# Attention block on one core: the third form of a row's bits made in place by an accumulating transfer from POOL, with 6 row buffers and 70 rows

## The chip, the core and the metric

The kernel runs on one core of a Trainium2 chip. The core has a matrix engine (PE, whose weight loads the profile lists apart as PEld), a vector engine (DVE), an engine for functions such as exp (ACT), a general engine (POOL) and an engine that only issues transfers (SP). Each runs its own list of instructions strictly in order, and before an instruction it can wait on semaphores that other engines or transfers raise. The metric is the device time of one execution in microseconds (us).

## The reference

The block is multi-head attention without a mask: 2048 positions, width 448, 16 heads of 28, all in bf16.

```
qkv = x @ wqkv                       # x: 2048 x 448, wqkv: 448 x 1344
q, k, v = split into 16 heads of 28
scores = q @ k^T * 28 ** -0.5        # per head 2048 x 2048
p = softmax(scores)
o = p @ v
return concat(o) @ wo                # wo: 448 x 448
```

## The kernel before

**Units, rows and tiles.** The work is cut into 16 units: a group g of four heads times a chunk c of 512 queries. A unit u walks over 16 blocks kt of 128 keys, and "row" r = 16u + kt is one such block: four tiles, one per head, each of 128 keys by 512 queries. There are 256 rows and 1024 tiles. For each tile PE computes scores into one bank of the PSUM memory (line 904, names S for groups of tiles and SD for single ones); then exp is taken; then PE multiplies the result with V and adds it up in one bank over the unit's 16 rows (line 871, names PV). A column of ones in V gives the softmax denominators. Four such products of a row, one per head, run side by side; they are called a pass here.

**Two ways to take exp.** Most rows go through ACT (line 966, names E): groups of 3 and 2 tiles alternate, over banks 0 to 2 and 3 to 4, and the results land in a ring PT of 43 slots. The rows listed in `PLAN["rows"]`, 67 of them, go through DVE instead. There exp is made from bits. Line 928 (names D1) clamps a tile's scores, adds a constant and writes 16-bit integers into a buffer DY whose bits, read as fp16, are a coarse exp. To even out the coarse error, line 936 (names DS0 and DS1) makes two more forms of the whole row by adding the integers 344 and 682, into DS. The row's product with V then has three terms in three passes: DY with V, the first DS with VW0 and the second DS with VW1, where VW0 and VW1 are V scaled by 101/128 and 80/128 (line 859). Such a row's four score tiles sit in banks 5 to 7, which also hold the accumulator and serve projections and outputs. Rows rotate through 3 buffers DY and 3 pairs DS.

**What sets the order.** The program is written as a list of operations with dependencies, priorities and guessed durations, and a list scheduler (`_Prog.schedule`) fixes each engine's order before the kernel is built. On PE every pass of products with V names the one before it in `after`, so that passes run in the order of the rows and terms. Where the scheduler sees PE falling idle it adds passes with zeros (line 484, name Z).

**Start and end.** POOL first fills parts of V, the padded `wop` and ONE with constants (lines 492 to 495); DVE makes the identity `id_b` and SEL (lines 460, 462 and 496) for the transposes of x (line 538). After a unit, its accumulator is copied (line 723) and normalised through a round trip of small transfers (lines 729 to 739). The last unit is normalised on PE and DVE (lines 778 to 839): two half copies (line 801), N1 (line 809), N2 (line 824), and the output projection of the last four tiles of positions in parts, OPA (line 789) and OPB (line 834). The output projections of other tiles of the last group (OP, line 710) are mixed in before.

Of the kernel before, what the change touches and what calls it, by code (L numbers as in the profile page):

```python
# [7 lines left out]
ALU = mybir.AluOpType  # L8
# [4 lines left out]
I16 = mybir.dt.int16  # L13
# [50 lines left out]
class _Prog:  # L64
# [272 lines left out]
PHASE = (0, 344, 682)  # L337
# [3 lines left out]
ZLO = -ZADD  # L341


CFG = {"late": 4.5, "load": 1.5, "load0": 18, "dcost": 2.3, "dlead": 30.385592406, "aslack": 235.147215477, "opp": 0.0, "oload": 2.5, "klead": 0.405674492, "vlag": 0.024622608, "hot1": 45000.0, "hotm": 3600.0, "nslack": 2585.717981114, "dlook": 20.0, "plook": 471.074451806, "rcost": 4.9, "rlead": 1.0, "rend": 4, "rgap": 2, "acost": 0.4455, "dprio": 0.651412491, "nride": 4, "rslack": 300.0, "stail": 24, "jprio": -0.750113813, "sdlap": 4.771128299, "vwlead": 1.249363626, "sdpen": 6.528606395, "rcostx": -0.000676632}

PLAN = {
    "rows": [9, 14, 16, 24, 26, 28, 33, 38, 41, 50, 53, 54, 57, 61, 62, 70, 72, 77, 80, 84, 88, 95, 97, 98, 103, 107, 109, 111, 113, 117, 123, 125, 131, 135, 138, 139, 141, 148, 149, 152, 162, 163, 164, 165, 169, 176, 177, 179, 180, 187, 189, 190, 193, 199, 200, 207, 211, 212, 213, 215, 222, 229, 231, 234, 235, 244, 248],
    "late": [1.281070854, 1.964014751, 1.915657661, 0.76, 2.743900482, 1.159356603, 1.904466413, 1.845975994, 2.106524837, 2.189415295, 2.428349574, 2.873971098, 2.728623137, 3.84085501, 2.733578841, 4.131340808, 3.508351422, 5.446684044, 4.832243098, 4.46548081, 5.163206443, 7.002171665, 6.90767575, 7.804407036, 4.947925744, 6.78739139, 5.302922841, 6.89552453, 9.777227448, 10.389677342, 7.735503962, 7.490566717, 8.23514301, 7.360578973, 7.83742904, 10.319692841, 8.329224918, 8.680463746],
}


def _fast(nc, x, wqkv, wo, out, n_heads=16):
# [12 lines left out]
    NQT = QCH // 128  # L365
    HC = H * 32
    GD = 4 * DH
    NPT = 43
    NDR = 3
    NDS = 3  # L370
    NPH = len(PHASE)
    NMENG = "dve"
    NOB = 4
# [14 lines left out]
    with es:  # L388
        def sb(name, shape, dt):
            return es.enter_context(nc.sbuf_tensor(name, shape, dt))  # L390
# [13 lines left out]
        DS = sb("DS", [128, NPH - 1, NDS, 2048], I16)  # L404
# [20 lines left out]
        def i32v(ap):  # L425
            return ap.bitcast(I32)
# [65 lines left out]
        ms_v0 = P.add("pool", lambda e: e.memset(V4[:, :, DH:32], 0.0), dur=1500, prio=-9, name="ms_v0")  # L492
        ms_v1 = P.add("pool", lambda e: e.memset(V4[:, :, VONE:VONE + 1], 1.0), deps=[ms_v0], dur=800, prio=-9, name="ms_v1")
        ms_wop = P.add("pool", lambda e: e.memset(i32v(wop.rearrange("p g d -> p (g d)")), 0), dur=900, prio=-8, name="ms_wop")
        ms_one = P.add("pool", lambda e: e.memset(ONE[:, :], 1.0), dur=100, prio=-7, name="ms_one")
        sel_op = P.add("dve", (lambda e: e.tensor_copy(SEL[:, :], id_f.rearrange("p (h r) -> p h r", r=32)[:, :, VONE])),
                       deps=[id_f_op], dur=100, prio=-6, name="sel")
# [344 lines left out]
        def pv(u, kt):  # L842
            g, c = units[u]
            r = u * NK + kt
            if r in n_row:
                ri = n_row[r] % NDR
                rk = n_row[r] % NDS
                terms = [DY[:, ri, :]] + [DS[:, k, rk, :] for k in range(NPH - 1)]
                parts = [[t_.bitcast(FP16)[:, h * 512:(h + 1) * 512] for h in range(4)] for t_ in terms]
                deps_of = [row_ops[r]] + [[o_] for o_ in row_ev[r]]  # L850
                slots = []
            else:
                slots = [tile_slot[(u, kt, h)] for h in range(4)]
                parts = [[PT[:, pi * 512:(pi + 1) * 512] for _, pi in slots]]
                deps_of = [list({id(tile_ev[(u, kt, h)]): tile_ev[(u, kt, h)] for h in range(4)}.values())]

            if r in n_row and (g, kt // 4) not in vw_ev:
                c4 = kt // 4
                vw_ev[(g, c4)] = [P.add("dve", (lambda e, k=k: e.tensor_scalar(VW[:, g % 2, k, 4 * c4:4 * c4 + 4, :], V[:, 4 * c4:4 * c4 + 4, g * 128:(g + 1) * 128],
                                                                              WTERM[k + 1], None, ALU.mult)),  # L860
                                        deps=[v_ev[(g, c4)], vw_used.get((g % 2, c4))], dur=200, prio=u + kt / NK - CFG["vwlead"], name=f"VW{k}_{g}_{c4}")
                                  for k in range(NPH - 1)]

            def weights(k, h):
                return V[:, kt, (4 * g + h) * 32:(4 * g + h + 1) * 32] if k == 0 else VW[:, g % 2, k - 1, kt, 32 * h:32 * h + 32]

            def f_pv(e, k, p_):
                ins = None
                b = pv_open[u].banks[0]
                for h in range(4):  # L870
                    ins = e.matmul(ps[32 * h:32 * h + 32, b * 512:(b + 1) * 512], weights(k, h), p_[h], start=(kt == 0 and k == 0), stop=(kt == NK - 1 and k == len(parts) - 1), tile_position=(0, 32 * h))  # L871
                return ins
            base_pr = (u - 60.0 if u == NU - 1 and kt >= NK - 3 else u + (kt + 4) / NK)
            for k, p_ in enumerate(parts):
                first, fin = kt == 0 and k == 0, kt == NK - 1 and k == len(parts) - 1
                op = P.add("pe", (lambda e, k=k, p_=p_: f_pv(e, k, p_)), deps=deps_of[k]
                           + [v_ev[(g, kt // 4)] if k == 0 else vw_ev[(g, kt // 4)][k - 1]], acq=(("M", 1) if first else None),
                           after=[last_pv[0]], kind="c", units=1.0, act=512.0, acc=(True if first else False if fin else None), prio=base_pr, name=f"PV{u}_{kt}" + (f"_{k}" if k else ""))
                last_pv[0] = op
                if first:  # L880
                    pv_open[u] = op
                if r in n_row:
                    row_pv[(n_row[r], k)] = op
                    if k:
                        vw_used[(g % 2, kt // 4)] = op
            for s_ in slots:
                slot_last[s_] = op
            if kt == NK - 1:
                (last_unit if u == NU - 1 else post_unit)(u, op)

        last_pv = [None]
        pv_next = 0
        done = set()
# [17 lines left out]
        def row_tile(r, h, partner, p_pr):  # L911
# [7 lines left out]
            old = row_pv.get((n_row[r] - NDR, 0))  # L919
            prev_row = row_at.get(n_row[r] - NDR, [])  # L920
# [5 lines left out]
            hold.append(s)  # L926
            s.ride = True
            o1 = P.add("dve", (lambda e, ri=ri, h=h, s=s: e.tensor_scalar(DY[:, ri, h * 512:(h + 1) * 512], bank(s.banks[0]), ZLO, ZADD, ALU.max, ALU.add)),  # L928
                       deps=[s, old] + prev_row, dur=600, prio=-90.0, name=f"D1_{r}_{h}", rel=[(s, 0)])
# [4 lines left out]
            rk = n_row[r] % NDS  # L934
            assert n_row[r] < NDS or (n_row[r] - NDS, 1) in row_pv, "DVE rows too close"
            row_ev[r] = [P.add("dve", (lambda e, k=k: e.tensor_scalar(DS[:, k, rk, :], DY[:, ri, :], float(PHASE[k + 1]), None, ALU.add)),  # L936
                               deps=row_ops[r] + [row_pv.get((n_row[r] - NDS, k + 1))], dur=600, prio=pr + 0.001 * k, name=f"DS{k}_{r}") for k in range(NPH - 1)]
            row_at[n_row[r]] = row_ev[r]
            done.update(4 * r + j for j in range(4))

        row_ev = {}
        row_at = {}
        for gi, (kind, idx, b0) in enumerate(items):
            tl = [tiles[i] for i in idx]
            w = len(tl)
# [32 lines left out]
            if todo_rows and 4 * todo_rows[0] - CFG["dlead"] <= idx[-1] and (nxt < NDS or (nxt - NDS, NPH - 1) in row_pv):  # L978
# [773 lines left out]
```

## Time and profile before

| | before |
|---|---|
| median of 3 runs | 362.63 us (362.26 to 363.6) |
| the profiled execution | 362.26 us, of which the span of instructions is 360.4 us |
| POOL busy | 3.4 us in 9 instructions, the last ending before 5 us |
| transfers | 9.91 MB, mean 27 GB/s over the span |
| granted PE clock | 1.000 |

The profile page gives for each engine the time with work in it (overlapping instructions counted once), the span in slices, the chain of waits that ended last, and groups of instructions with their mean duration. Queries of the trace give the same for stretches of the span, the instructions in order of time, and who waited for whom.

### The profile page before, as it was taken

The numbers are of one execution on the slowest core, as the hardware profiler recorded it, in microseconds if no ns is written. First come the engines' busy times: TensorE is split into PE (matmuls) and PEld (weight loads), VectorE is DVE, ScalarE is ACT, GpSimd is POOL, SyncE is SP. The second block draws the span as 40 slices with busy tenths as digits, with TensorE's granted clock in tenths as the row PEclk, the third lists the DMA queues.
The fourth block names the chain that finished last, engine by engine and source line by source line (L and its number), as shares of the span: only waits on it lengthen the run. The fifth ranks groups of instructions, "written<-read, shape, count | busy, mean of one in ns | idle before, by whom it ended". The sixth has DMA issues, their size and how long they took to land.

```text
span 360.4 us, 8848 instructions
## 1 busy us (share of the span) xinstructions
PE 342.2 (95%) x3885; PEld 114.4 (32%) x3885; DVE 321.8 (89%) x574; ACT 345.5 (96%) x307; POOL 3.4 (1%) x9
## 2 busy tenths in 40 slices
PE   8999999999999999999999999999998989999996
PEld 4444322332223243223333323332222222234323
DVE  6579999798999999999999998999999999999504
ACT  2999999999999999999999999999999999999992
POOL 3000000000000000000000000000000000000000
PEclk9999999999999999999999999999999999999999
DMA  8600000100100000000000000000000001010201
GB/s 232 152 2 3 2 32 5 32 2 3 33 0 5 32 18 17 2 32 3 20 15 5 31 2 32 3 14 22 29 4 3 20 15 32 16 44 28 78 29 54
DMA packets 13940, 9.91 MB, mean 27 GB/s; under 512 B 7504, under 2 KB 12048, under 8 KB 13896
## 3 DMA queue, kind: packets, MB, share of 16 engines
q1 hardware_dynamic: 13096, 8.74, 8.4%
q8 instruction: 31, 0.51, 0.6%
q10 hardware_dynamic: 800, 0.56, 0.5%
q14 instruction: 13, 0.11, 0.1%
HBM read 7.23 MB, written 2.06 MB: 26 GB/s over the span
## 4 chain that ended last, share of the span: by engine, by line
ACT 88%; PE 11%; issue 0%; ACTq 0%; DVE 0%
ACT PT L966 87%; PE ps L904 3%; PE ps L871 2%; PE ps L555 2%; PE ps L484 1%; PE ps L789 1%; PE ps L572 0%; PE ps L538 0%; ACT OUTS L696 0%; PE ps L824 0%; PE ps L758 0%; PE ps L809 0%; PE ps L769 0%; PE ps L710 0%; ACT QT L524 0%
## 5 line engine op out<-in xcount | busy, mean ns | idle before, releaser
L966 ACT ACTIVATE PT<-ps 128x1536 bf16<-128x1536 f32 (+1 forms) x303 | 342.5, 1398 | 1.0 <-PE ps L904 0.9
L928 DVE TENSOR_SCALAR DY<-ps 128x512 int16<-128x512 f32 x268 | 175.4, 685 | 9.3 <-PE ps L904 8.1
L904 PE MATMUL ps<-QT,KT 28*128 28x512 bf16 x1024 | 151.6, 384 | 12.9 <-ACT PT L966 8.4
L936 DVE TENSOR_SCALAR DS<-DY 128x2048 int16<-128x2048 int16 x134 | 89.9, 683 | 0.4
L904 PEld LDWEIGHTS ps<-QT,KT 28*128 28x128 bf16 x1024 | 39.7, 91 | 139.0 <-ACT PT L966 101.5
L871 PE MATMUL ps<-PT,V 128*32 128x512 bf16 x756 | 65.8, 385 | 0.7 <-DVE OTS L723 0.4
L871 PE MATMUL ps<-DS,VW 128*32 128x512 f16 x536 | 49.3, 385 | 0.1
L555 PE MATMUL ps<-xT,w_raw 112*32 112x512 bf16 x512 | 35.8, 381 | 0.0
L484 PE MATMUL ps<-ZM,ZW 128*32 128x512 bf16 x324 | 29.5, 410 | 1.2 <-DVE ZM L466 1.2
L871 PE MATMUL ps<-DY,V 128*32 128x512 f16 x268 | 26.5, 385 | 0.1
L871 PEld LDWEIGHTS ps<-PT,V 128*32 128x32 bf16 x756 | 17.1, 94 | 28.4 <-issue 21.9
L871 PEld LDWEIGHTS ps<-DS,VW 128*32 128x32 bf16 x536 | 12.5, 94 | 20.5 <-issue 13.7
L572 PE MATMUL ps<-w_raw,xT 112*128 112x112 bf16 x256 | 17.1, 214 | 0.0
L555 PEld LDWEIGHTS ps<-xT,w_raw 112*32 112x32 bf16 x512 | 12.2, 95 | 13.1 <-issue 3.8
L698 DVE CAST OUTS<-ps 128x448 bf16<-128x448 f32 x14 | 8.6, 622 | 7.6 <-PE ps L710 7.2
L572 PEld LDWEIGHTS ps<-w_raw,xT 112*128 112x128 bf16 x256 | 13.0, 98 | 6.7 <-issue 4.7
L528 DVE CAST KT<-ps 128x512 bf16<-128x512 f32 x16 | 11.0, 689 | 3.5 <-PE ps L555 3.4
L484 PEld LDWEIGHTS ps<-ZM,ZW 128*32 128x32 bf16 x324 | 7.8, 99 | 13.6 <-issue 10.9
L528 DVE CAST V<-ps 128x448 bf16<-128x448 f32 x16 | 9.9, 621 | 2.0 <-PE ps L572 1.9
L526 DVE TENSOR_SCALAR QT<-ps 128x512 bf16<-128x512 f32 x15 | 10.3, 686 | 1.5 <-PE ps L555 1.5
L710 PE MATMUL ps<-wop,XO 128*128 128x448 bf16 x48 | 11.5, 355 | 0.0
L723 DVE COPY OTS<-ps 128x512 f32<-128x512 f32 x15 | 10.3, 687 | 0.5 <-PE ps L871 0.5
(49 smaller groups left out, 79.2 us busy)
## 6 DMA issues: line engine op xcount, KB each, us to landing
RB<-scr_r SPq DMA_DIRECT2D x14, 256.0 KB
out_dram<-OUTS SPq DMA_DIRECT2D x14, 112.0 KB, 1.7
XO<-in_x_dram SPq DMA_DIRECT2D x3, 448.0 KB, 6.3
w_raw<-in_wqkv_dram SPq DMA_DIRECT2D x5, 196.0 KB, 6.3
wop<-in_wo_dram SPq DMA_DIRECT2D x16, 24.5 KB
XO<-in_x_dram SPq DMA_DIRECT2D x1, 224.0 KB, 3.5
XO<-in_x_dram ACTq DMA_DIRECT2D x1, 224.0 KB, 4.0
scr_l<-OTS SPq DMA_DIRECT2D x14, 8.0 KB
```

The costliest lines, as they stand in the source:

```text
L484: ins = e.matmul(ps[32 * h:32 * h + 32, b * 512:(b + 1) * 512], ZW[:, :], ZM[:, :], start=shut, stop=shut, skip_group_check=not shut, tile ...
L526: fe = (lambda e: e.tensor_scalar(evac[0](), evac[1](hold[0].banks[0]), mul, None, ALU.mult))
L528: fe = (lambda e: e.tensor_copy(evac[0](), evac[1](hold[0].banks[0])))
L555: ins = e.matmul(ps[32 * h:32 * h + 32, b * 512:(b + 1) * 512], w_raw[0:IT, it, col:col + 32], xT[0:IT, it, c * 512:(c + 1) * 512], start= ...
L572: ins = e.matmul(ps[:, b * 512 + j * GD:b * 512 + (j + 1) * GD], xT[0:IT, it, n * 128:(n + 1) * 128], w_raw[0:IT, it, 2 * D + g * GD:2 * D ...
L710: return e.matmul(bank(hold[0].banks[0])[:, 0:D], OTN[:, gg, n * 128:(n + 1) * 128], wop[:, gg, :], start=(gg == 0), stop=(gg == G - 1))
L723: accev = P.add("dve", (lambda e: e.tensor_copy(OTS[:, ub, :], bank(pv_open[u].banks[0]))), deps=[last_pv, ots_last[ub]], dur=610, prio=pr ...
L871: ins = e.matmul(ps[32 * h:32 * h + 32, b * 512:(b + 1) * 512], weights(k, h), p_[h], start=(kt == 0 and k == 0), stop=(kt == NK - 1 and k ...
L904: ins = e.matmul(bank(b), KT[32 * h:32 * h + rows, g, kt * 128:(kt + 1) * 128], QT[32 * h:32 * h + rows, g, c * QCH:(c + 1) * QCH], start= ...
L928: o1 = P.add("dve", (lambda e, ri=ri, h=h, s=s: e.tensor_scalar(DY[:, ri, h * 512:(h + 1) * 512], bank(s.banks[0]), ZLO, ZADD, ALU.max, AL ...
L936: row_ev[r] = [P.add("dve", (lambda e, k=k: e.tensor_scalar(DS[:, k, rk, :], DY[:, ri, :], float(PHASE[k + 1]), None, ALU.add)), deps=row_ ...
L966: ex = P.add("act", (lambda e, p0=p0, w=w, bf=bf: e.activation(PT[:, p0 * 512:(p0 + w) * 512], bank(bf(), w), AF.Exp, scale=ESCALE)), deps ...
```

## The change

Three things are changed together, and the tables of rows and of scheduling parameters are replaced by others.

The second DS of a row is no longer made in a buffer of its own. Once the first term's pass has read DY (and DS0 has been made from it), 682 is added to DY in place, and the third pass reads DY again. For rows with kt below 11 (`KDMA`) the addition is an accumulating transfer that POOL issues: the destination is DY, the source a constant tile PHC of 128 x 2048 integers 682, filled once by POOL. Its pass gets a priority of 5 key blocks later (`PVBACK`). For kt of 11 and above, DVE adds 682 in place (line 904 of the changed kernel).

A pass with V now waits only for the unit's first pass, and the unit's last one for all of them, so that passes of a unit can change places. DY gets 6 buffers instead of 3, DS keeps 3 single ones, and PT has 39 slots instead of 43. The list of rows on DVE has 70 entries instead of 67: 44 with kt below 11 and 26 above.

```diff
-    "rows": [9, 14, 16, 24, 26, 28, 33, 38, 41, 50, 53, 54, 57, 61, 62, 70, 72, 77, 80, 84, 88, 95, 97, 98, 103, 107, 109, 111, 113, 117, 123, 125, 131, 135, 138, 139, 141, 148, 149, 152, 162, 163, 164, 165, 169, 176, 177, 179, 180, 187, 189, 190, 193, 199, 200, 207, 211, 212, 213, 215, 222, 229, 231, 234, 235, 244, 248],
+    "rows": [11, 15, 17, 19, 21, 31, 32, 37, 38, 48, 52, 53, 56, 60, 63, 68, 70, 75, 76, 80, 82, 93, 95, 97, 98, 102, 103, 109, 110, 114, 115, 119, 124, 129, 131, 136, 139, 143, 145, 147, 159, 160, 162, 169, 171, 173, 178, 179, 181, 183, 190, 191, 196, 200, 203, 204, 205, 210, 215, 216, 217, 221, 223, 225, 229, 233, 239, 244, 245, 255],
...
-    NPT = 43
-    NDR = 3
+    NPT = 39
+    NDR = 6
     NDS = 3
+    KDMA = 11
+    PVBACK = 5
+    ADDB = 1310720
...
+        PHC = sb("PHC", [128, 2048], I16)
...
         ms_wop = P.add("pool", lambda e: e.memset(i32v(wop.rearrange("p g d -> p (g d)")), 0), dur=900, prio=-8, name="ms_wop")
+        ms_phc = P.add("pool", lambda e: e.memset(PHC[:, :], PHASE[2]), dur=1800, prio=-7.5, name="ms_phc")
         ms_one = P.add("pool", lambda e: e.memset(ONE[:, :], 1.0), dur=100, prio=-7, name="ms_one")
...
-                terms = [DY[:, ri, :]] + [DS[:, k, rk, :] for k in range(NPH - 1)]
+                terms = [DY[:, ri, :], DS[:, n_row[r] % NDS, :], DY[:, ri, :]]
...
-                           after=[last_pv[0]], kind="c", units=1.0, act=512.0, acc=(True if first else False if fin else None), prio=base_pr, name=f"PV{u}_{kt}" + (f"_{k}" if k else ""))
+                           after=[last_pv[0]] if first else unit_pv[u] if fin else [pv_open[u]], kind="c", units=1.0, act=512.0, acc=(True if first else False if fin else None),
+                           prio=pr_, name=f"PV{u}_{kt}" + (f"_{k}" if k else ""))
...
+            for k, p_ in enumerate(parts):
+                if k == 2:
+                    d_ = [row_pv[(n_row[r], 0)]] + row_ev[r]
+                    if kt < KDMA:
+                        add = P.add("pool", (lambda e: e.dma_start(DY[:, ri, :], PHC[:, :], accum_op=ALU.add)), deps=d_ + [ms_phc], dur=1000, prio=base_pr,
+                                    name=f"ADD{r}", dma_group=grp_add[ri], nbytes=ADDB)
+                    else:
+                        add = P.add("dve", (lambda e: e.tensor_scalar(DY[:, ri, :], DY[:, ri, :], float(PHASE[2]), None, ALU.add)), deps=d_, dur=600,
+                                    prio=base_pr - 0.5, name=f"DS1_{r}")
+                    deps_of[2] = [add]
+                op = term(k, p_, base_pr + (PVBACK / NK if k == 2 and kt < KDMA else 0.0))
...
-            row_ev[r] = [P.add("dve", (lambda e, k=k: e.tensor_scalar(DS[:, k, rk, :], DY[:, ri, :], float(PHASE[k + 1]), None, ALU.add)),
-                               deps=row_ops[r] + [row_pv.get((n_row[r] - NDS, k + 1))], dur=600, prio=pr + 0.001 * k, name=f"DS{k}_{r}") for k in range(NPH - 1)]
+            row_ev[r] = [P.add("dve", (lambda e: e.tensor_scalar(DS[:, rk, :], DY[:, ri, :], float(PHASE[1]), None, ALU.add)),
+                               deps=row_ops[r] + [row_pv.get((n - NDS, 1))], dur=600, prio=pr, name=f"DS0_{r}")]
```

What the new order is shows at three places. The first is the end of PE's program. These rows of the kernel before run from the last scores (line 904) to the first step of the normalisation (line 809); line 871 is a pass with V of the last unit, 484 zeros, 789 the parts OPA:

```order
L904 MATMUL ps<-QT,KT 128x512 x3
L484 MATMUL ps<-ZM,ZW 32x512 x12
L871 MATMUL ps<-PT,V 32x512 x4
L789 MATMUL ps<-wop,XO 128x448 x5
L871 MATMUL ps<-PT,V 32x512 x4
L789 MATMUL ps<-wop,XO 128x448 x3
L809 MATMUL ps<-SEL,OTS 128x4 x4
```

In the changed kernel the same stretch (scores at line 928, passes at 876, OPA at 794, N1 at 814, and output projections OP of other tiles at 715) reads:

```order
L928 MATMUL ps<-QT,KT 128x512 x4
L715 MATMUL ps<-wop,XO 128x448
L876 MATMUL ps<-PT,V 32x512 x8
L794 MATMUL ps<-wop,XO 128x448 x7
L876 MATMUL ps<-PT,V 32x512 x4
L794 MATMUL ps<-wop,XO 128x448
L715 MATMUL ps<-wop,XO 128x448 x8
L876 MATMUL ps<-DY,VW 32x512 x4
L876 MATMUL ps<-PT,V 32x512 x12
L876 MATMUL ps<-DY,VW 32x512 x4
L814 MATMUL ps<-SEL,OTS 128x4 x4
```

Before, the last row of the last unit is on ACT and its pass is the last of the unit, with one row's pass and five parts ahead of it. Now row 255 is on DVE; the pass of row 254 (the single `PT,V x4` in the middle), which waits for ACT's last exp, has nine projection products and five passes behind it and ahead of N1.

The second place is a row in the middle of PE's program whose third form comes by transfer, row 97. Its first two passes, `DY,V` and `DS,VW`, stand ahead of these rows; its third pass is the last row here:

```order
L560 MATMUL ps<-xT,w_raw 32x512 x16
L928 MATMUL ps<-QT,KT 128x512 x4
L876 MATMUL ps<-DY,V 32x512 x4
L928 MATMUL ps<-QT,KT 128x512 x3
L876 MATMUL ps<-DS,VW 32x512 x4
L876 MATMUL ps<-PT,V 32x512 x4
L928 MATMUL ps<-QT,KT 128x512 x4
L876 MATMUL ps<-PT,V 32x512 x8
L928 MATMUL ps<-QT,KT 128x512 x4
L876 MATMUL ps<-DY,V 32x512 x4
L876 MATMUL ps<-DS,VW 32x512 x4
L876 MATMUL ps<-DY,VW 32x512 x4
```

Before, none to four groups of scores stood between a row's first and third pass, one in 36 of 67 rows. Now the third stands behind the next row's first two, with four groups of scores after its own second pass and six after its own first. Over the 44 rows with a transfer, 6 (2 rows), 7 (14 rows), 8 (8 rows) or 9 and more (20 rows) groups of scores stand between the first pass and the third; between the second and the third 4 (2 rows), 5 (1 row), 6 (10 rows) or 7 and more (31 rows).

The third place is POOL's program, which ended with ONE before. The constant for the transfers stands between `wop` and ONE, and the 44 transfers follow:

```order
L496 MEMSET V 128x256x4
L497 MEMSET V 128x256
L498 MEMSET wop 128x896
L499 MEMSET PHC 128x2048
L500 MEMSET ONE 128x1
L901 DMA DY<-PHC 128x2048 x44
```

Each transfer waits for its row's first pass on PE and for DS0 on DVE. In all the engines' lists, ACT now has 298 exps instead of 303, DVE 280 instead of 268 of D1 and 96 instead of 134 of DS (26 of them in place), and PE 592 instead of 599 passes of products, zeros and projections of q and k (68 instead of 81 of zeros).

More of the change, by code (lines that the diff above doesn't have):

```diff
@@ L349 @@
+    "late": [1.287831187, 1.867734824, 1.28739526, 1.125307774, 2.594606463, 1.25476838, 2.26330289, 1.9814921, 2.01934556, 2.411528998, 2.78757281, 4.040943142, 3.207888019, 3.478414581, 4.56312649, 4.086335713, 4.295360609, 4.49380888, 4.596174152, 4.654962379, 5.084795196, 5.603283679, 6.068422443, 6.150428236, 5.487154907, 7.421494728, 5.090395608, 5.901719011, 9.81260526, 7.771657427, 7.823620963, 7.500366806, 7.511986723, 7.285049906, 7.709176179, 9.727966012, 8.078105838, 7.981302912],
 }
@@ L403, in _fast @@
         DY = sb("DY", [128, NDR, 2048], I16)
[L404 removed]
+        DS = sb("DS", [128, NDS, 2048], I16)
+        PHC = sb("PHC", [128, 2048], I16)
         OTS = sb("OTS", [128, 2, 512], FP32)
@@ L846, in pv @@
                 ri = n_row[r] % NDR
-                rk = n_row[r] % NDS
-                terms = [DY[:, ri, :]] + [DS[:, k, rk, :] for k in range(NPH - 1)]
+                terms = [DY[:, ri, :], DS[:, n_row[r] % NDS, :], DY[:, ri, :]]
                 parts = [[t_.bitcast(FP16)[:, h * 512:(h + 1) * 512] for h in range(4)] for t_ in terms]
-                deps_of = [row_ops[r]] + [[o_] for o_ in row_ev[r]]
+                deps_of = [row_ops[r], row_ev[r], []]
                 slots = []
@@ L858, in pv @@
                 c4 = kt // 4
+                used = vw_used.pop((g % 2, c4), [])
                 vw_ev[(g, c4)] = [P.add("dve", (lambda e, k=k: e.tensor_scalar(VW[:, g % 2, k, 4 * c4:4 * c4 + 4, :], V[:, 4 * c4:4 * c4 + 4, g * 128:(g + 1) * 128],
                                                                               WTERM[k + 1], None, ALU.mult)),
-                                        deps=[v_ev[(g, c4)], vw_used.get((g % 2, c4))], dur=200, prio=u + kt / NK - CFG["vwlead"], name=f"VW{k}_{g}_{c4}")
+                                        deps=[v_ev[(g, c4)]] + used, dur=200, prio=u + kt / NK - CFG["vwlead"], name=f"VW{k}_{g}_{c4}")
                                   for k in range(NPH - 1)]
@@ L872, in f_pv, with term @@
                 return ins
-            base_pr = (u - 60.0 if u == NU - 1 and kt >= NK - 3 else u + (kt + 4) / NK)
-            for k, p_ in enumerate(parts):
+            final = u == NU - 1 and kt >= NK - 3
+            base_pr = u - 60.0 if final else u + (kt + 4) / NK
+            def term(k, p_, pr_):
                 first, fin = kt == 0 and k == 0, kt == NK - 1 and k == len(parts) - 1
-                op = P.add("pe", (lambda e, k=k, p_=p_: f_pv(e, k, p_)), deps=deps_of[k]
+                op = P.add("pe", (lambda e: f_pv(e, k, p_)), deps=deps_of[k]
                            + [v_ev[(g, kt // 4)] if k == 0 else vw_ev[(g, kt // 4)][k - 1]], acq=(("M", 1) if first else None),
-                           after=[last_pv[0]], kind="c", units=1.0, act=512.0, acc=(True if first else False if fin else None), prio=base_pr, name=f"PV{u}_{kt}" + (f"_{k}" if k else ""))
-                last_pv[0] = op
+                           after=[last_pv[0]] if first else unit_pv[u] if fin else [pv_open[u]], kind="c", units=1.0, act=512.0, acc=(True if first else False if fin else None),
+                           prio=pr_, name=f"PV{u}_{kt}" + (f"_{k}" if k else ""))
+                unit_pv.setdefault(u, []).append(op)
                 if first:
                     pv_open[u] = op
+                if fin:
+                    last_pv[0] = op
                 if r in n_row:
@@ L884, in pv @@
                     if k:
-                        vw_used[(g % 2, kt // 4)] = op
+                        vw_used.setdefault((g % 2, kt // 4), []).append(op)
+                return op
+            for k, p_ in enumerate(parts):
[9 more added lines that the diff above has]
+                op = term(k, p_, base_pr + (PVBACK / NK if k == 2 and kt < KDMA else 0.0))
             for s_ in slots:
@@ L889, in pv @@
                 (last_unit if u == NU - 1 else post_unit)(u, op)
+        unit_pv = {}
+        grp_add = [_DmaGroup(f"add{i}") for i in range(NDR)]
         last_pv = [None]
@@ L918, in row_tile @@
             ri = n_row[r] % NDR
-            old = row_pv.get((n_row[r] - NDR, 0))
-            prev_row = row_at.get(n_row[r] - NDR, [])
+            old = row_pv.get((n_row[r] - NDR, 2))
             assert n_row[r] < NDR or old is not None, "DVE rows too close"
@@ L933, in row_tile @@
             pr = r / NK - 0.2 + CFG["dprio"]
-            rk = n_row[r] % NDS
-            assert n_row[r] < NDS or (n_row[r] - NDS, 1) in row_pv, "DVE rows too close"
-            row_ev[r] = [P.add("dve", (lambda e, k=k: e.tensor_scalar(DS[:, k, rk, :], DY[:, ri, :], float(PHASE[k + 1]), None, ALU.add)),
-                               deps=row_ops[r] + [row_pv.get((n_row[r] - NDS, k + 1))], dur=600, prio=pr + 0.001 * k, name=f"DS{k}_{r}") for k in range(NPH - 1)]
-            row_at[n_row[r]] = row_ev[r]
+            n = n_row[r]
+            rk = n % NDS
+            row_ev[r] = [P.add("dve", (lambda e: e.tensor_scalar(DS[:, rk, :], DY[:, ri, :], float(PHASE[1]), None, ALU.add)),
+                               deps=row_ops[r] + [row_pv.get((n - NDS, 1))], dur=600, prio=pr, name=f"DS0_{r}")]
             done.update(4 * r + j for j in range(4))
         row_ev = {}
-        row_at = {}
         for gi, (kind, idx, b0) in enumerate(items):
@@ L977, in _fast @@
             nxt = len(n_row) - (1 if todo_rows and todo_rows[0] in n_row else 0)
-            if todo_rows and 4 * todo_rows[0] - CFG["dlead"] <= idx[-1] and (nxt < NDS or (nxt - NDS, NPH - 1) in row_pv):
+            if todo_rows and 4 * todo_rows[0] - CFG["dlead"] <= idx[-1] and (nxt < NDS or (nxt - NDS, 1) in row_pv) and (nxt < NDR or (nxt - NDR, 2) in row_pv):
                 r = todo_rows[0]
```

5 lines of the change are left out of this document (2 added, 3 removed).

## The prediction

> **What bounds the kernel now.** I read the page's busy times first, then the chain of waits, then stretches of the trace.
>
> ```profile
> PE 342.2 (95%) x3885; PEld 114.4 (32%) x3885; DVE 321.8 (89%) x574; ACT 345.5 (96%) x307; POOL 3.4 (1%) x9
> ACT 88%; PE 11%; issue 0%; ACTq 0%; DVE 0%
> ACT PT L966 <- PE ps L904: 0.9, 2, 0.5
> 0.00:9.42 9.42, 8.09 (x93) 3.92 (x93) 6.07 (x12) 1.88 (x2) 3.44 (x9) 1.00 0.86 239
> 9.42:352.45 343.03, 329.31 (x3737) 107.68 (x3736) 312.10 (x551) 342.50 (x303) 0.00 (x0) 1.00 0.07 21
> 352.45:360.40 7.95, 4.79 (x57) 2.79 (x56) 3.63 (x12) 1.09 (x3) 0.00 (x0) 1.00 0.19 61
> ```
>
> The last three lines are stretches: length, then busy time and count of PE, PEld, DVE, ACT and POOL, clock, share of the transfer engines and GB/s. From 9.42 to 352.45 us ACT runs its 303 exps and is busy 342.50 of 343.03 us; in the whole run it waited for scores 0.9 us. So the span is a start of 9.42, a stream of 343.03 that ACT sets, and an end of 7.95. The other engines have little to spare inside the stream: 13.7 us on PE, 30.9 on DVE. The execution took 362.26 us, 1.86 more than its span and 0.37 less than the median of 362.63; sums go against 362.26.
>
> **Part 1, three more rows on DVE: ACT's stream gets shorter.** 303 exps over 756 tiles take 343.03 us: 151 pairs of groups of 3 and 2, and one single tile.
>
> ```profile
> L966 ACT ACTIVATE PT<-ps 128x1536 bf16<-128x1536 f32 x151 | 243.2, 1611 | 1.0 <-PE ps L904 0.9
> L966 ACT ACTIVATE PT<-ps 128x512 bf16<-128x512 f32 x1 | 0.7, 728 | 0.0
> 345.02 7.43 ACT L966 ACTIVATE PT<-ps 128x1536 bf16<-128x1536 f32 x7
> ```
>
> Durations overlap at their ends, so the stream gives the price: 343.03 / 756 = 0.4537 us a tile, 343.03 / 303 = 1.132 a group. Twelve tiles leave ACT: **-5.45 us**, if the others keep up.
>
> They should on average. PE loses 7 passes. The chain's PE pieces show four passes in 0.98 and two in 0.55, so 0.215 each: 1.5 us less, and five groups of scores less.
>
> ```profile
> 163.72 0.55 PE ps L871 x8
> 179.64 0.98 PE ps L871 x16
> L928 DVE TENSOR_SCALAR DY<-ps 128x512 int16<-128x512 f32 x268 | 175.4, 685 | 9.3 <-PE ps L904 8.1
> L936 DVE TENSOR_SCALAR DS<-DY 128x2048 int16<-128x2048 int16 x134 | 89.9, 683 | 0.4
> ```
>
> DVE gains 12 of D1 and loses 38 of DS. The groups' busy times, with overlaps counted once, give 175.4 / 268 = 0.654 and 89.9 / 134 = 0.671. That is +7.9 and -25.5, so 17.6 us less, off the path. It also gets a new wait: the in-place addition of 26 rows waits for a pass on PE, with D1s queued behind it and PE's single scores waiting for those D1s' banks. It mostly stands two or more instructions behind DS0, and I cost it at nothing; if it stalls 0.2 us each time, DVE has the 5 us.
>
> **Part 2, the new end.** Before, ACT's last exp ends at 352.45:
>
> ```profile
> 351.10 0.40 PE L871 MATMUL ps<-PT,V 128*32 128x512 bf16 x4 [0.19 <-ACT PT L966]
> 351.43 1.12 PE L789 MATMUL ps<-wop,XO 128*128 128x448 bf16 x5
> 352.50 0.40 PE L871 MATMUL ps<-PT,V 128*32 128x512 bf16 x4
> 352.96 0.76 DVE L801 COPY OTS<-ps 128x256 f32<-128x256 f32 x2 [6.38 <-PE ps L871]
> 330.59 0.86 PE ps L710 x4
> ```
>
> One pass follows (to 352.90), then the copy and the rest: 0.45 us from ACT to the full accumulator. In the new order the pass that needs ACT's last exp has nine projection products and five passes behind it, all ahead of the copy that waits for the unit's last pass. The next instruction can start 0.33 after a pass (351.10 to 351.43). Products take 0.215 (0.86 for four), passes 0.215: 0.05 + 0.33 + 9 x 0.215 + 5 x 0.215 + 0.1 for the last one to drain is 3.5. The seven products ahead of it run while ACT works on its last 3 + 1 tiles, and don't count. The rest, 7.5 us, stays. So **+3.0 us**.
>
> **Part 3, the 44 transfers.** No transfer from POOL stands in the trace. From its neighbours:
>
> ```profile
> LT<-scr_l SPq DMA_DIRECT2D x14, 8.0 KB, 1.6
> scr_r<-RS SPq DMA_DIRECT2D x14, 8.0 KB, 1.4
> 0.00:11.00 11.00, 9.67 (x117) 4.76 (x117) 6.84 (x14) 3.46 (x4) 3.44 (x9) 1.00 0.91 248
> L494 POOL MEMSET wop<- 128x896 int32 x1 | 1.2, 1164 | 0.0
> L493 POOL MEMSET V<- 128x256 bf16 x1 | 1.2, 1237 | 0.1
> ```
>
> A small transfer lands 1.4 to 1.6 us after issue. At 91% busy the engines moved 248 GB/s, so 273 when full: 524 KB takes 1.92 us for one crossing, 5.8 if constant, row and result go one after the other. POOL's own share lies between nothing and its longest row, 1.24. So 1.4 + 1.92 = 3.3 us to 1.6 + 5.8 + 1.24 = 8.6; I take two crossings (two reads, the write beside them) and 1.16: 1.4 + 3.84 + 1.16 = 6.4. The room in PE's order is at least 6 groups of scores after the first pass, at 1.132 us each 6.8, and 7.9 in 14 rows more. DS0 is a second condition; counted from its pass the smallest room is 4 groups, 4.5 us, though DS0 itself is done earlier. At 6.4 the stalls sum to 0 by the first count and 4.5 by the second. I take **+0.5 us**. PE waits with everything behind it in its list, the next scores first, and ACT has at most two groups in banks, so a stall passes on nearly whole.
>
> The Trainium skill ("DMA: Bandwidth & Descriptors", Anatomy of one DMA) fits transfers issued this way as 2.0 us plus bytes over 436 GB/s. For 524 KB that is 3.2 us, an estimate from that page for a plain copy; by it no row would stall and the 0.5 would be 0. No run here shows it yet.
>
> **Sum.** 362.26 - 5.45 + 3.0 + 0.5 = **360.3 us**, 0.6% below the median.
>
> **The rivals.**
>
> *A later start.*
>
> ```profile
> 2.01 1.24 POOL L493 MEMSET V<- 128x256 bf16 x1
> 2.06 2.01 DVE L462 CAST id_b<-id_f 128x128 bf16<-128x128 f32 x1
> 2.21 1.87 DVE L496 COPY SEL<-id_f 128x4 f32<-128x4 f32 x1
> 2.83 1.16 POOL L494 MEMSET wop<- 128x896 int32 x1
> 3.93 0.19 POOL L495 MEMSET ONE<- 128x1 bf16 x1
> 4.79 1.59 PE L538 MATMUL ps<-id_b,XO 128*112 128x128 bf16 x16
> L733 DVE RECIPROCAL RS<-LT 128x16 f32<-128x16 f32 x14 | 3.4, 244 | 0.0
> L492 POOL MEMSET V<- 128x1024 bf16 x1 | 1.0, 951 | 0.0
> ```
>
> A copy of four columns took 1.87 us on DVE beside POOL's memsets, where 16 columns take 0.244 elsewhere; it and the identity came free at 4.07, when `wop` was done. PHC stands right behind `wop`. At 951 ns for 1024 elements it takes 1.9 us; if DVE stays shut out until then, the identity is ready at 5.97 and the transposes start at about 6.05 instead of 4.79: +1.3, **361.6 us**. For it: DVE did not get in between L493 and L494. Against: it got in before ONE was over, which stands where PHC will stand. Chance 0.22.
>
> *POOL shuts DVE out in the stream.* The same rows say it: if each transfer's preparation keeps DVE's additions in SBUF waiting, DVE loses time 44 times. DVE has 30.9 + 17.6 = 48.5 us to spare, 1.1 us a transfer; below that the time stays within 3 us of the sum (363.3 at most, from single scores that come late), above it DVE becomes the bound. A full 1.24 each time is 54.6 us, 6 more than there is: 366. But only what works within SBUF as the copies above do would meet it, 96 of DS and 32 of VW, not the 280 of D1, which read PSUM. Chance 0.10. The Trainium skill has this as a rule ("SBUF — State Buffer", Who interferes with whom): DVE in its two-port modes and POOL, which writes the descriptors of such transfers, lock each other out of a shared pair of ports, and it advises against hiding such a transfer under DVE work. By that rule, the 2.01 and 1.87 us here agree.
>
> *Transfers land too late (the other side).* Place: PE's third pass of the 44 rows. It decides from about 7 us per transfer: at 8 us the shortfall over all rows, counted from the first pass, is 3.5 us (363.3 with the sum's other terms), at the upper bound of 8.6 it is 13.1 (372.9), and counted from the DS pass more. For it: two conditions, POOL's share unknown, six groups the smallest room. Against: the middle of my bounds is below. Chance 0.22.
>
> *The end isn't longer,* because PE gets through the late passes while ACT finishes, or the products take less: 362.26 - 5.45 + 0.5 = 357.3. Against it: the order is fixed. Chance 0.06.
>
> **How the numbers follow.** The forecast has 0.40. A measurement of this kernel can tell some 0.5% from no change, so the bounds are 360.8 and 364.4 around the median. Faster: 0.36 of the forecast (its stalls can reach 1 us and more, which puts 0.04 into the middle) and 0.06 from the unchanged end, 0.42. Same: 0.04, the later start 0.22, 0.07 of the shut-out DVE and 0.03 of transfers late by little, 0.36. Slower: 0.19 of late transfers and 0.03 of the DVE case, 0.22. The range runs from 357.5 to 368: below it lies the unchanged end in part, above it the late transfers beyond 8.3 us, some 0.17 together.
>
> **What will show it.** Right: ACT's stream near 337.6 us with under 1.5 us of waiting for scores; first exp at 9.4; from ACT's last exp to the half copies (L801 of before) 3.5 us; PE's waits for transfers at the DY,VW passes below 1 us in total. The later start would show as a first exp at 10.7 and an identity ready near 6; late transfers as waits of PE on DMA of whole microseconds and exps waiting behind them; a shut-out DVE as DS durations far above 683 ns. Wrong altogether I'd be if the accumulating transfer runs at a fraction of the rate seen at the start, or if so much more traffic makes the small transfers of the normalisation late, which DVE would then wait for.

## The result and the profile after

| | before | after |
|---|---|---|
| median of 8 executions each | 362.44 us (361.88 to 363.6) | 365.06 us (363.53 to 366.58) |
| after over before | | 1.0073, 95% interval 1.0051 to 1.0096 |
| the profiled execution, its span | 362.26 us, 360.4 us | 366.52 us, 364.6 us |
| granted PE clock, mean | 1.000 | 0.988 (0.988 to 0.996 over the executions) |

The change makes the kernel 0.7% slower. Medians here and below are over all executions, while ratios and ranges leave out single executions that a lower clock made several us longer. The profiled execution of after is among its longest, 1.5 us above its median.

Lines of after's page: busy times, two groups of instructions, and the new transfers (KB each, median us to landing).

```profile
PE 341.6 (94%) x3857; PEld 116.5 (32%) x3857; DVE 311.0 (85%) x548; ACT 339.9 (93%) x302; POOL 44.8 (12%) x54
L987 ACT ACTIVATE PT<-ps 128x1536 bf16<-128x1536 f32 (+1 forms) x298 | 337.0, 1411 | 1.1 <-PE ps L928 1.1
L959 DVE TENSOR_SCALAR DS<-DY 128x2048 int16<-128x2048 int16 x70 | 48.4, 691 | 1.0
DY<-PHC POOLq DMA_DIRECT2D x44, 512.0 KB, 5.2
```

And the three stretches of the prediction (start, ACT's stream of exps, end), with the columns as there:

```profile
0.00:9.24 9.24, 7.51 (x93) 3.56 (x93) 6.07 (x12) 1.88 (x2) 5.17 (x10) 1.00 0.87 243
9.24:346.77 337.53, 323.78 (x3683) 107.48 (x3682) 300.00 (x523) 336.97 (x298) 39.65 (x44) 1.00 0.43 89
346.77:364.60 17.83, 10.31 (x83) 5.50 (x82) 4.91 (x14) 1.09 (x2) 0.00 (x0) 0.75 0.12 41
```

The start is 0.18 us shorter, the stream 5.50 (343.03 to 337.53), and the end 9.88 longer (7.95 to 17.83): together +4.2, the difference of the spans. The whole loss stands behind ACT's last exp, with a mean PE clock of 0.75.

The end in three stretches: ACT's last exp to the first half copy; from there to the end of FLAG, DVE's last instruction; from FLAG to the end of the program. First before, then after:

```profile
352.45:352.96 0.51, 0.51 (x6) 0.22 (x6) 0.00 (x1) 0.00 (x1) 0.00 (x0) 1.00 0.00 0
352.96:357.85 4.89, 4.28 (x52) 2.58 (x50) 3.62 (x12) 0.92 (x2) 0.00 (x0) 1.00 0.02 5
357.85:360.40 2.55, 0.00 (x0) 0.00 (x0) 0.00 (x1) 0.17 (x1) 0.00 (x0) 1.00 0.53 180
```

```profile
346.77:352.05 5.28, 3.45 (x34) 1.34 (x33) 1.16 (x2) 0.00 (x0) 0.00 (x0) 1.00 0.08 26
352.05:360.02 7.97, 6.87 (x49) 4.17 (x49) 3.74 (x13) 1.09 (x2) 0.00 (x0) 0.57 0.12 40
360.02:364.60 4.58, 0.00 (x0) 0.00 (x0) 0.00 (x0) 0.00 (x0) 0.00 (x0) 0.77 0.18 60
```

All three grew: by 4.77, 3.08 and 2.03 us. In the first, PE works for 3.45 us and then has nothing to do. The instructions of DVE and PE around it, of after and then of DVE of before, in order of time:

```profile
348.31 0.62 DVE L703 CAST OUTS<-ps 128x448 bf16<-128x448 f32 x1 [2.83 <-PE ps L715]
349.83 0.39 PE L876 MATMUL ps<-DY,VW 128*32 128x512 f16 x4
351.51 0.62 DVE L703 CAST OUTS<-ps 128x448 bf16<-128x448 f32 x1 [2.58 <-issue]
352.05 0.74 DVE L806 COPY OTS<-ps 128x256 f32<-128x256 f32 x2
352.52 1.87 PE L814 MATMUL ps<-SEL,OTS 128*128 128x4 f32 x8 [2.30 <-DVE OTS L806]
```

```profile
341.96 0.62 DVE L698 CAST OUTS<-ps 128x448 bf16<-128x448 f32 x1 [2.18 <-PE ps L710]
345.96 0.62 DVE L698 CAST OUTS<-ps 128x448 bf16<-128x448 f32 x1 [3.37 <-PE ps L710]
```

Each engine's program branches once to a last block of code. DVE's branch by the view of that source line, of after and of before (three durations in ns, then its start):

```profile
L1697 DVEq COMPARE_BRANCH  x1: 80/80/80, 348.3 to 348.3; - x1
```

```profile
L1676 DVEq COMPARE_BRANCH  x1: 80/80/80, 342.0 to 342.0; - x1
```

The accumulator is full at 350.22, but DVE's next instruction after the branch at 348.3, the eviction OPEV11 (the copy of a projection's result out of PSUM), starts only at 351.51, and no other engine is named as holding it ("issue"). Before, that eviction had to wait for PE until 345.96 in any case. Because the nine projection products now run so late, DVE reaches the branch late, and the branch is in the way. PE meanwhile idles 2.30 us. Behind that its products take about double: N1 1.87 us for eight in place of 1.05 (line 814, and 809 before).

The last piece is POOL's final drain at the end of the program (of after; before it took 45 ns):

```profile
L1679 POOLq DRAIN  x1: 3663/3663/3663, 360.8 to 360.8; - x1
L1679 SPq DRAIN  x1: 13/13/13, 361.9 to 361.9; - x1
```

In the kernel before, SP was the last engine to be done. Here SP is done at 361.9, and the program waits for POOL until 364.5.

So the reading is: order on PE +3.0 (accumulator full 3.45 us after ACT's end, not 0.45), branch +1.77, slow PE +3.08, drain +2.03. The runs below test the last three, and ask whether the first can be had for less.

### The profile page after: what moved, and what is told of

It reads as the page before. It is cut to its first block, busy times and chain, and to the rows that moved or that the text cites. A ratio compares the mean times of both kernels' runs of the same rounds, so it can differ in the third digit from the quotient of the medians.

```text
span 364.6 us, 8841 instructions
## 1 busy us (share of the span) xinstructions
PE 341.6 (94%) x3857; PEld 116.5 (32%) x3857; DVE 311.0 (85%) x548; ACT 339.9 (93%) x302; POOL 44.8 (12%) x54
## 4 chain that ended last, share of the span: by engine, by line
ACT 90%; PE 6%; issue 1%; DMA 1%; DVE 1%; DVEq 0%
ACT PT L987 90%; DMA XO<-in_x_dram 1%; PE ps L794 1%; PE ps L876 1%; PE ps L928 1%; PE ps L560 1%; PE ps L814 1%; PE ps L829 1%; PE ps L839 0%; DVE OUTS L703 0%; PE ps L715 0%; PE ps L774 0%; PE ps L763 0%; PE ps L488 0%; PE ps L543 0%
## 5 line engine op out<-in xcount | busy, mean ns | idle before, releaser
L987 ACT ACTIVATE PT<-ps 128x1536 bf16<-128x1536 f32 (+1 forms) x298 | 337.0, 1411 | 1.1 <-PE ps L928 1.1
L951 DVE TENSOR_SCALAR DY<-ps 128x512 int16<-128x512 f32 x280 | 182.8, 681 | 15.4 <-PE ps L928 13.7
L928 PE MATMUL ps<-QT,KT 28*128 28x512 bf16 x1024 | 148.0, 384 | 12.9 <-ACT PT L987 6.5
L901 POOL DMA_DIRECT2D DY<-PHC x44 | 39.6, 908 | 285.7 <-PE ps L876 149.5
L876 PE MATMUL ps<-PT,V 128*32 128x512 bf16 x744 | 68.6, 386 | 0.5 <-DVE DY L951 0.4
L959 DVE TENSOR_SCALAR DS<-DY 128x2048 int16<-128x2048 int16 x70 | 48.4, 691 | 1.0
L876 PE MATMUL ps<-DS,VW 128*32 128x512 f16 x280 | 27.7, 385 | 0.0
L876 PEld LDWEIGHTS ps<-PT,V 128*32 128x32 bf16 x744 | 17.6, 94 | 30.0 <-issue 23.8
L876 PE MATMUL ps<-DY,VW 128*32 128x512 f16 x280 | 26.9, 386 | 0.0
L488 PE MATMUL ps<-ZM,ZW 128*32 128x512 bf16 x272 | 24.8, 409 | 1.2 <-DVE ZM L470 1.2
L904 DVE TENSOR_SCALAR DY<-DY 128x2048 int16<-128x2048 int16 x26 | 17.7, 680 | 0.3 <-PE ps L876 0.2
```

The costliest lines, as they stand in the source:

```text
L901: add = P.add("pool", (lambda e: e.dma_start(DY[:, ri, :], PHC[:, :], accum_op=ALU.add)), deps=d_ + [ms_phc], dur=1000, prio=base_pr, name ...
L904: add = P.add("dve", (lambda e: e.tensor_scalar(DY[:, ri, :], DY[:, ri, :], float(PHASE[2]), None, ALU.add)), deps=d_, dur=600, prio=base_ ...
L928: ins = e.matmul(bank(b), KT[32 * h:32 * h + rows, g, kt * 128:(kt + 1) * 128], QT[32 * h:32 * h + rows, g, c * QCH:(c + 1) * QCH], start= ...
L959: row_ev[r] = [P.add("dve", (lambda e: e.tensor_scalar(DS[:, rk, :], DY[:, ri, :], float(PHASE[1]), None, ALU.add)), deps=row_ops[r] + [ro ...
L987: ex = P.add("act", (lambda e, p0=p0, w=w, bf=bf: e.activation(PT[:, p0 * 512:(p0 + w) * 512], bank(bf(), w), AF.Exp, scale=ESCALE)), deps ...
```

## The experiments

Expectations are set against 365.1 us for after.

**The branch moved.** In `_fast`, DVE's branch stands one eviction earlier; all orders stay.

```diff
-        P.JUMP_AT = {"pe": "PV8_11", "dve": f"OPEV{n0 - 1}", ...
+        P.JUMP_AT = {"pe": "PV8_11", "dve": f"OPEV{n0 - 2}", ...
```

> The branch of VectorE's program to its tail stands one eviction earlier (ahead of OPEV10 in place of OPEV11); every order stays as in the changed kernel. Theory (the branch is exposed there, PE then idles 2.3 us and its clock falls for the rest): the 1.8 us of late half copies and most of the 3.1 us of slow tail go, about 360.2 us against 365.1 for the changed kernel, granted clock over 0.9 in the last 12 us. Rival A (OPEV11 waited for a free output buffer, not for its program): 365.1, the half copies as late as before. Rival B (the clock falls from something else than the idle PE, such as the transfers): 363.3, half copies on time, clock near 0.7 at the end.

Measured: median 364.28 us (362.91 to 366.08), ratio 1.0062 (1.0039 to 1.0085); the profiled execution 362.97, 3.55 less than after's. DVE's branch in that run, its evictions behind it, and the end's three stretches with two from the stream:

```profile
L1697 DVEq COMPARE_BRANCH  x1: 80/80/80, 346.2 to 346.2; - x1
```

```profile
349.64 1.38 DVE L703 CAST OUTS<-ps 128x448 bf16<-128x448 f32 x2 [2.83 <-PE ps L715]
```

```profile
286.00:288.00 2.00, 1.96 (x18) 0.56 (x18) 1.27 (x3) 2.00 (x2) 0.00 (x0) 0.64 0.07 24
288.00:290.00 2.00, 2.00 (x15) 0.34 (x11) 1.26 (x3) 1.54 (x2) 0.86 (x1) 0.51 0.43 134
...
348.10:351.61 3.51, 3.45 (x34) 1.34 (x33) 1.25 (x3) 0.00 (x1) 0.00 (x0) 1.00 0.11 38
351.61:356.51 4.90, 3.80 (x49) 2.48 (x49) 3.62 (x12) 0.93 (x2) 0.00 (x0) 1.00 0.07 23
356.51:361.20 4.69, 0.00 (x0) 0.00 (x0) 0.00 (x0) 0.16 (x1) 0.00 (x0) 0.68 0.31 101
```

The branch now lies under a wait for PE, OPEV10 and OPEV11 run back to back, and the output buffers (rival A) held nothing up. The first stretch is 1.77 shorter, the second 3.07, which are the two terms. But the start and the stream came out 1.33 us longer in this execution (9.72 and 338.38); some 3.4 us of the stream, between 286 and 290, ran at half the PE clock though PE was busy. The median fell by only 0.8 us, against 4.9 expected: part of that is that after's profiled execution, from which the terms come, lies 1.5 us above its median; what else the other executions lost stays open, since only one of each kernel has a trace.

**Zeros in PE's gap.** Ten passes of zeros behind the last pass, nothing else.

```diff
+            def f_zs(e):
+                b = open_ops[0][1][0].banks[0]
+                for _ in range(10):
+                    for h in range(4):
+                        ins = e.matmul(ps[32 * h:32 * h + 32, b * 512:b * 512 + D], ZW[:, :], ZM[:, 0:D], start=False, stop=False, ...)
+                return ins
+            zs = P.add("pe", f_zs, deps=[ms_z], after=[last_pv, open_ops[0][2]], dur=100, prio=pr, name="ZS")
...
-                n1s.append(P.add("pe", f_n1, deps=[evs[k], sel_op], after=n1s[-1:], ...
+                n1s.append(P.add("pe", f_n1, deps=[evs[k], sel_op], after=n1s[-1:] or [zs], ...
```

> Ten passes of zeros (40 products, about 2.1 us) stand on PE between the last pass with V and N1, added into a projection bank, so that PE doesn't idle while it waits for the half copies; nothing else changes. Theory (idling lowers the clock): half copies as late as in the changed kernel, but the stretch from them to the flag about 4.8 us in place of 7.8: 362.1 us. Rival B (the clock falls for another reason): 365.1 or a little more, the stretch still 7.8 us.

Measured: 363.38 us (363.0 to 363.91), ratio 1.0029 (1.0017 to 1.004); the profiled execution 363.46, 3.06 under after's. Its first two stretches:

```profile
347.05:352.06 5.01, 5.01 (x74) 2.42 (x73) 1.16 (x2) 0.00 (x1) 0.00 (x0) 1.00 0.10 31
352.06:356.95 4.89, 4.14 (x57) 2.48 (x49) 3.62 (x13) 0.92 (x2) 0.00 (x0) 1.00 0.07 23
```

The half copies are still late, as they should be, but the second stretch is 4.89, that of before, at full clock. PE's idling is what lowered the clock; the transfers were the same. All six executions had a clock of 0.997 to 0.999, after's eight 0.988 to 0.996. The median fell by 1.7 us and not by the 3.0 expected: after's profiled execution, from which the 3.08 comes, is among its longest.

**The planner's tail drawn wider.** More passes of the last unit are pushed behind, and its third passes drawn forward, so that the projection's tiles 10 and 11 are done inside ACT's stream.

```diff
-            final = u == NU - 1 and kt >= NK - 3
+            final = u == NU - 1 and kt >= NK - 13
...
-                op = term(k, p_, base_pr + (PVBACK / NK if k == 2 and kt < KDMA else 0.0))
+                op = term(k, p_, -45.0 if u == NU - 1 and k == 2 else base_pr + (PVBACK / NK if k == 2 and kt < KDMA else 0.0))
```

> The planner's rule for the last tiles of the last unit is drawn wider (last 13 tiles in place of 3) and the last unit's third passes are drawn forward, so that between the last pass that waits for ACT and N1 there stand one pass and one product in place of 5 passes and 9 products; the projection's tiles 10 and 11 are done before ACT's last exps. Theory: accumulator full 0.6 us after ACT's end in place of 3.45 (-2.9), and since VectorE then reaches its branch some 4 us earlier in ACT's stream, the branch is covered (-1.8) and PE doesn't idle (-3.1): about 357.3 us. If the order alone counts and the branch stays exposed: 362.2 us. Rival B (clock falls in any case): 360.4 us.

Measured: 364.34 us (364.04 to 366.08), ratio 1.0067 (1.0051 to 1.0082): missed by 7 us. ACT's waits in that run, its stream, and the end's first two stretches:

```profile
ACT PT L987 <- PE ps L928: 3.8, 4, 2.0
ACT PT L987 <- PE ps L876: 1.8, 1, 1.8
```

```profile
9.54:351.95 342.41, 328.89 (x3727) 109.29 (x3726) 301.54 (x525) 337.26 (x298) 39.73 (x44) 1.00 0.43 87
351.95:352.67 0.72, 0.72 (x10) 0.22 (x9) 0.00 (x0) 0.00 (x1) 0.00 (x0) 1.00 0.33 118
352.67:357.60 4.93, 4.30 (x54) 2.58 (x53) 3.63 (x12) 0.93 (x2) 0.00 (x0) 1.00 0.04 11
```

The end does what was expected, 0.72 and 4.93 us. But the stream is 4.88 longer: ACT now waits 5.6 us for PE in place of 1.1. All but 0.5 us of it comes between 330 and 347 us. So in this order the work that left the end is paid in the last part of the stream. My expectation had counted it there at nothing.

**POOL drained early.**

```diff
             F.emit_engine(e, eng, fs, jump)
+            if e == "pool":
+                eng.drain()
```

> POOL executes a drain right behind its last transfer, some 30 us before the end, where it has nothing else to do. Theory (the 3.66 us of the final drain are POOL's settling of its transfers): the early drain takes the 3.7 us unseen, the final one under 0.2 us, 363.0 us. Rival (the time belongs to the program's end, such as the code behind the branch, whatever was issued before): the final drain stays at 3.7 us, 365.1 us.

Measured: 363.72 us, ratio 1.0027 (1.0015 to 1.004); the profiled execution 362.89. The early drain and the final one, and the end's second and third stretches:

```profile
L1715 POOLq DRAIN  x1: 6398/6398/6398, 331.0 to 331.0; - x1
L1679 POOLq DRAIN  x1: 45/45/45, 359.3 to 359.3; - x1
```

```profile
352.09:358.59 6.50, 5.42 (x49) 3.29 (x49) 3.69 (x13) 1.09 (x2) 0.00 (x0) 0.74 0.08 28
358.59:361.10 2.51, 0.00 (x0) 0.00 (x0) 0.01 (x1) 0.00 (x0) 0.00 (x0) 0.90 0.48 162
```

The last stretch is that of before (2.51 against 2.55). The 2.0 us belong to the transfers, not to the program's end; a run without any transfer (below) ends with 45 ns too. The second stretch is 1.47 shorter than after's as well; that is the clock, taken up in the last section.

**Branch and drain together**, the two edits above.

> Both the earlier branch of VectorE (as in the run that moved it) and POOL's early drain. Theory (branch, clock and drain are separate terms): FLAG as early as with the branch alone (some 356.5 us in the trace), the final drain 45 ns, so about 361 us in the profiled run, 2.1 under that run; its executions may still scatter over 3 us like those of the branch alone (362.9 to 366.1), since about 0.5 us of PE idling is left before N1. If the drain's gain was only another phase of the clock: no gain over the branch alone, 364.3 us.

Measured: 360.59 us, ratio 0.9941 (0.9922 to 0.9961), the profiled execution also 360.59. Its end, from ACT's last exp to the end of the program:

```profile
347.86:358.80 10.94, 7.25 (x83) 3.82 (x82) 4.88 (x14) 1.09 (x2) 0.00 (x0) 1.00 0.19 65
```

In the traces the terms add up: the end is 10.94 in place of 17.83, so 6.89 less, and 1.77 + 3.08 + 2.03 is 6.88. (The first exp came 1.1 us later in this execution, at 10.34.) In the ratios they don't: the branch alone was worth 0.1% of the time and the drain alone 0.5%, both together 1.3%. So whatever else the executions with the branch alone lost is gone here too; why is not shown.

**With three passes of zeros**, `range(3)` in place of `range(10)`.

> As the one with branch and drain, and three passes of zeros (12 products, about 0.6 us) on PE ahead of N1 where 0.5 us of idling is left. Theory (what scatters is the PE clock, which falls after idling): executions within 1 us of each other, granted clock 0.997 or more in each, median about 361.0 us, under the kernel before by 0.4%. If the scatter has another cause (the transfers, the start): executions over 3 us as with the branch alone, median 361.5 to 362.5.

Measured: 359.79 us (359.51 to 360.19), ratio 0.993 (0.9915 to 0.9944). Stream and end of that run, the end's three stretches behind:

```profile
9.41:346.92 337.51, 323.83 (x3683) 107.64 (x3682) 300.16 (x523) 336.95 (x298) 39.74 (x44) 1.00 0.44 89
346.92:350.43 3.51, 3.51 (x42) 1.59 (x45) 1.25 (x2) 0.01 (x1) 0.00 (x0) 1.00 0.12 38
350.43:355.34 4.91, 4.28 (x61) 2.56 (x53) 3.63 (x12) 0.93 (x2) 0.00 (x0) 1.00 0.08 27
355.34:357.90 2.56, 0.00 (x0) 0.00 (x0) 0.00 (x0) 0.15 (x1) 0.00 (x0) 0.80 0.53 179
```

The executions lie within 0.7 us of each other, at clocks of 0.999 and 1.0; with branch and drain alone they lay between 359.32 and 361.42, at 0.994 to 1.0. This kernel is faster than before and after. Its gain over the one without zeros (0.8 us in the medians) is not beyond the intervals.

**No transfers.** `KDMA = 0` instead of 11: DVE makes all 70 third forms.

> All 70 third forms are made in place by VectorE (a setting of the kernel, KDMA = 0), none by a transfer; the planner orders PE and VectorE anew. Theory (the transfers carry 44 instructions of 0.68 us that VectorE has no room for): VectorE's busy time goes from 311 to about 341 us and the stream of exps or its end waits for it, 367 to 378 us though the final drain is 45 ns; the small transfers (scr_l to LT) land in 1.6 us again in place of 3.5. Rival (VectorE has room, the transfers only cost): 362 us or less.

Measured: ratio 1.0455 (1.0398 to 1.0512), median 386.06 us. The only trace is of an execution of 386.8 us with a mean clock of 0.955. From it: ACT's waits, the stretch from ACT's last exp to the half copy, and a transfer:

```profile
ACT PT L987 <- PE ps L928: 13.1, 11, 3.6
```

```profile
363.24:377.46 14.22, 12.87 (x127) 4.63 (x127) 8.82 (x15) 0.00 (x0) 0.00 (x0) 1.00 0.18 59
```

```profile
LT<-scr_l SPq DMA_DIRECT2D x14, 8.0 KB, 1.6
```

By the ratio, which rests on two executions (376.42 and 381.33), that is about 379 us (1.0455 x 362.3), just above the range expected, and the rival falls: with these 70 rows and this plan the transfers earn more than they cost. Whether a plan made for DVE alone would lose as much isn't tested; the kernel before, with 67 rows and no transfer, takes 362. Where the time goes is not shown either. DVE's busy time is 334.2 us, less than the 341 expected. ACT does wait for scores, but 11 of its 13.1 us lie between 210 and 242 us, where this execution ran at half the PE clock. What stands outside that is the end: 14.22 us at full clock from ACT's last exp to the half copy, against 5.28 in after, with PE still at passes, projections and scores for 12.87 of them. Small transfers land in 1.6 us again; after had 3.5.

## Why the prediction failed

- **Part 1 held.** Predicted -5.45 us for the stream and under 1.5 us of waiting for scores; measured -5.50 and 1.1. The chance given to a DVE that stalls came to nothing: DVE's busy time fell by 10.8 us, less than my 17.6 (its groups give 182.8 + 48.4 + 17.7 - 175.4 - 89.9 = -16.4, but they overlap each other less), and that didn't hold the stream up: 1.1 us is all that ACT waited for scores.
- **Part 2 failed, in one clause: "The rest, 7.5 us, stays."** The clause ahead of it was right: 3.5 us from ACT's end to the full accumulator, measured 3.45. But the rest, 7.5 us before, grew to 14.38. The step that failed is that it followed PE's list alone to the copy and took all that stands behind it, on every engine, as unchanged. Added were 1.77 for a branch that had lain under a wait, 3.08 for a PE clock that fell in the gap so made, and 2.03 for POOL's drain. Runs show each: with the branch moved the first two go, with zeros in the gap only the second, with the early drain the third.
- **Part 3: the size too large, the mechanism in part.** Landing took 5.2 us against 6.4 of my estimate. No wait of PE on a POOL transfer stands in after's trace (at most 0.9 us in the other runs with transfers), so the 0.5 us was 0. Two full crossings, 3.84 us, are not borne out. Of after's page, the queue of these transfers (packets, MB, share of 16 engines' span):

```profile
q0 software_dynamic: 6336, 23.07, 33.4%
```

That is a third of 364.6 us; over 44 transfers it is 2.77 us each, more than one crossing at the start's rate (1.92) and less than two. With 1.4 for a small transfer and the 0.86 that POOL took that makes 5.0, an estimate close to the 5.2. The Trainium skill's fit ("DMA: Bandwidth & Descriptors", Anatomy of one DMA), 3.2 us for a plain copy of that size, was too low for this addition by 2.0.
- **The rivals.** *Later start:* no. PHC's memset took 1.89 us on POOL from 3.94, but SEL's copy was over at 4.09 as before and the first exp came at 9.24. *POOL shuts DVE out:* no; DS took 691 ns against 683, 0.6 us in 70. The rule of the Trainium skill that had spoken for it ("SBUF — State Buffer", Who interferes with whom) has no price here beyond those 0.6 us. *Too late:* no. *The end isn't longer:* no. None of them was what happened; "slower" came from a place that I had priced with one number.
- The sum itself comes true once the three terms are taken away: the kernel with branch, drain and zeros ran in 359.66 us under the profiler, against 360.3 predicted. Most of the difference is the 0.5 us for late transfers, which nothing took.

What could have been seen: the branch was in the trace of before, at 342.0, under a wait that the change moves. That POOL's drain would cost anything could not be read there.

## What to carry to other kernels

When a change moves what stands at the end of a critical stream, follow every engine's list to the end, with its branches and drains, and ask for each what hid it before. Price a wait that idles PE with what runs behind it at half clock, and fill it with zeros where it can't go. If a kernel begins to issue transfers from POOL, drain POOL while it is idle, not at the end.

## What the runs showed of the hardware

The PE clock stays at half for a whole number of equal steps. Stretches around the gap, of after and of the run with the early drain; the clock is the third column from the end:

```profile
348.90:352.20 3.30, 1.32 (x21) 0.44 (x20) 0.72 (x3) 0.00 (x0) 0.00 (x0) 1.00 0.12 40
352.20:352.40 0.20, 0.00 (x0) 0.00 (x0) 0.20 (x2) 0.00 (x0) 0.00 (x0) 0.63 0.00 0
352.40:359.00 6.60, 6.48 (x48) 4.09 (x48) 2.72 (x10) 0.54 (x1) 0.00 (x0) 0.50 0.06 20
359.00:359.20 0.20, 0.20 (x2) 0.00 (x0) 0.00 (x0) 0.16 (x1) 0.00 (x0) 0.80 0.00 0
```

```profile
353.70:353.90 0.20, 0.20 (x5) 0.15 (x8) 0.17 (x2) 0.00 (x0) 0.00 (x0) 0.72 0.00 0
353.90:357.10 3.20, 3.20 (x37) 1.84 (x35) 1.27 (x5) 0.14 (x1) 0.00 (x0) 0.50 0.02 5
357.10:357.30 0.20, 0.20 (x2) 0.15 (x1) 0.00 (x0) 0.20 (x1) 0.00 (x0) 0.75 0.00 0
```

Worked out from the mixed stretches, half clock lasted from 352.25 to 359.08, 6.83 us, and from 353.79 to 357.20, 3.41: two steps and one. The dip of the run with the branch moved (286.56 to 289.96) is one step as well. The one of the run without transfers, by stretches of 0.2 us at its ends (0.77 from 210.00, 0.93 from 240.80), lasted from 210.11 to 240.83, 30.72 us: nine. The same gap of 2.1 to 2.3 us thus cost 3.08 us in one execution and 1.61 in the other (6.50 against 4.89), which fits that after's executions scatter over 3 us. The fall came 2.0 us after the gap's start in the one (350.22) and 3.3 us in the other (350.45). The Trainium skill ("TensorE: Matmul & The Clock Gate", Part 1) tells of free-running windows of about 3.4 us, which agrees with the steps and with a fall that isn't tied to the gap's start. It also tells of a fall after an idle window, which asks for more than was needed here: 2.3 us of idling, with 1.32 us of work in the 3.30 ahead of the fall, were enough. Why the clock fell at 286.56 in the run with the branch moved is not shown: PE was at work for 2.87 of the 3.40 us ahead.

Also new: a transfer that adds 512 KB within SBUF lands in 5.2 us and takes 0.86 us of POOL's time (medians), and the drain behind the last one 6.4 us when it follows at once, still 3.66 when it comes 30 us later. Beside these transfers the small ones of the normalisation take 3.5 us in place of 1.6; nobody waited for them. A branch of DVE to its last block costs about 3.1 us where nothing covers it (348.39 to 351.51).
